# Block-diagonal attention scores on 32x32 tiles, row sums by TensorE, one range check, and a re-tuned schedule

**Chip, cores, metric.** One core of one Trainium2 chip. The metric is device time in microseconds (us), lower is better. Every run also notes the mean granted clock of TensorE. A run is called slow when it lies over 1.5% above the fastest of the same kernel on that chip, and fast otherwise; ratios use fast runs.

## The reference

```python
# x [4, 12480, 128] f32, inducing [32, 128] f32
def mab(q, kv):
    s = (q @ kv.transpose(0, 2, 1)) / sqrt(128)
    a = exp(s - s.max(-1, keepdims=True))
    a /= a.sum(-1, keepdims=True) + 1e-09
    return a @ kv
h = mab(I, x)            # 32 queries pool all 12480 tokens of a batch
y = mab(x, h)            # every token then attends to the 32 results
hid = y.reshape(49920, 128) @ w_in                        # [128, 2048]
out = (maximum(hid, 0) + alpha * minimum(hid, 0)) @ w_out # [2048, 128]
```

`h` of a batch needs all of its tokens, so each batch is gone through twice: once to pool it, once for its outputs. In between stands the **fold**: `h` and the feed-forward weights become small matrices that the outputs use. The kernel keeps the tokens of a batch on the chip between the two passes, so that `x` is read once.

## The kernel before

There are 28 chunks, seven per batch, six of 2048 tokens and one of 192. A full chunk is loaded by GpSimd's queue (f32 in memory, bf16 on arrival: the page shows 27.73 MB read and 13.83 MB in that queue's packets), turned round by VectorE in 32x32 squares ("flipped"), scored by TensorE, put through exp by ScalarE, flipped again and summed into `h`. After the fold, the same flipped tokens are scored against `h` (second scores), put through exp, and each of the chunk's four output tiles is summed from five matmuls (four of 128 columns, one of 512). An output tile is scaled either by VectorE straight from PSUM, or copied by ScalarE and scaled by GpSimd.

The order of every engine's instructions is fixed when the kernel is built. A planner inside the kernel plays the whole run with an estimated duration for each task, and the order in which tasks start in that play is the order in which the instructions are written out:

```python
RINGS = dict(xn=8, xt=14, p=7, h=1, e1=3, e1t=3, g=3, ob=4)   # buffers
CAPS = dict(A=3, S=3, F=7, O=6)                               # PSUM slots by use
SLACK, FILL, LATE, AP, BIAS = 1.5, 0.5, 70.0, 0.0, 0.8
PW, FB = 16.5, 3.0
TA, TS, TB, WL, LEAD = 3.6, 1.2, 4.2, 6, 2                    # deadlines = priorities
def dl_a(b, i): return 2.0 * i if b == 0 else 18.0 + TA * (NCK * (b - 1) + i)
# ... dl_s, dl_b alike

add(("PE", 0.02 + 4 * max(c.w / 2400, 0.06)), scores, [tf] + t_blk,
    take=["p:A"], prio=prio)      # engine and planned us, function, what it waits for,
                                  # buffers, priority
# ... Plan.play(): at each moment the ready task of the best priority starts,
#     its end is start + planned duration, and (engine, task) goes into the order
```

The parts that the change replaces (cuts marked):

```python
def blocks(a, eng, dst, flat):        # four copies put 32-row blocks on the diagonal
    rows = slice(a * M, (a + 1) * M)  # of a zeroed [128, 2, 4, 32, 2] weight tile
    copy(eng, dst[rows, :, a]..., flat[rows])

def scores(_):                        # first scores; the second use BH[r] for blkI
    for n, (bb, e) in enumerate(((0, 0), (0, 1), (1, 0), (1, 1))):
        nc.tensor.matmul(sc, blkI[:, bb, :, :, e]..., xT[:, :, bb, :, e],
                         start=(n == 0), stop=(n == 3))      # 128x128 weights, 512 columns

nc.scalar.activation(out=e1, in_=sc, func=EXP, scale=scale,
                     accum_out=esum[:, s.b, c.i : c.i + 1])  # first exp, with row sums
nc.scalar.activation(out=e2, in_=sc, func=EXP, scale=scale,
                     bias=centre[: c.p])                     # second exp

def f_flip(_):                        # fold: transpose to PSUM, then blocks() to BH[r]
    nc.vector.transpose(out=v["h4t"], in_=v["h4"]...)

def seal(_):                          # range check, once per batch
    nc.vector.tensor_scalar(out=odd, in0=odd, scalar1=~0x30003, op0=bitwise_and)
    nc.vector.tensor_reduce(out=odds[:, b : b + 1], in_=odd, op=max)
    nc.vector.memset(odd, 0)
```

The softmax here doesn't subtract the row's maximum and nothing guards it: scores larger than these inputs give would overflow.

Of the kernel before, what the change touches and what calls it, by code (L numbers as in the profile page):

```python
# [16 lines left out]
P = 128  # L17
M = 32
# [10 lines left out]
RINGS = dict(xn=8, xt=14, p=7, h=1, e1=3, e1t=3, g=3, ob=4)  # L29
CAPS = dict(A=3, S=3, F=7, O=6)  # L30
# [23 lines left out]
SLACK = 1.5  # L54
FILL = 0.5
LATE = 70.0
AP = 0.0
BIAS = 0.8


class Plan:
# [25 lines left out]
    def moved(self, now):  # L87

        while True:
            heads = {k: q[0] for k, q in self.queues.items() if q}  # L90
            busy = {k: h for k, h in heads.items() if h["begin"] <= self.clock + 1e-9}
            rate = {k: self.RATE[k] * (self.SHARE[k] if len(busy) == 2 else 1.0) for k in busy}
            events = [self.clock + h["left"] / rate[k] for k, h in busy.items()]
            events += [h["begin"] for k, h in heads.items() if k not in busy]
            nxt = min(events, default=1e9)
            to = min(nxt, now)
            for k, h in busy.items():
                h["left"] -= rate[k] * (to - self.clock)
                if h["left"] < 1.0:
                    h["end"] = to + 0.7  # L100
                    self.queues[k].pop(0)
            self.clock = max(self.clock, to)
            if nxt > now:
                return nxt

    def play(self):
# [4 lines left out]
        todo = list(self.tasks)  # L111
        self.order = order = []
        while todo:
            todo.sort(key=lambda t: (t["prio"], t["n"]))
# [3 lines left out]
            for t in todo:  # L118
                if any(d["end"] is None for d in t["deps"]):
                    continue  # L120
# [56 lines left out]
                todo.remove(t)  # L177
                order.append((choice, t))
                started = True
                break  # L180
            if not started:
                assert min(nxt) < 1e8, [(t["fn"].__name__, t["prio"], t["take"]) for t in todo if all(d["end"] is not None for d in t["deps"])][:20]
                now = min(nxt)
# [19 lines left out]
def kernel(  # L203
# [39 lines left out]
    def filler(n):  # L243
        p = ring("p")
        for _ in range(n):
            nc.tensor.matmul(
                p[:], blkI[:, 0, :, :, 0].rearrange("p a m -> p (a m)"), blkI[:].rearrange("p b a m e -> p (b a m e)"),
                start=True, stop=True,
            )
# [45 lines left out]
    blkI = const.tile([P, 2, G, M, 2], bf16, name="blkI")  # L295
    def blocks(a, eng, dst, flat):

        rows = slice(a * M, (a + 1) * M)
        copy(eng, dst[rows, :, a].rearrange("p b m e -> p b (m e)").bitcast(f32), flat[rows])
# [5 lines left out]
    def zeros(_):  # L305
        nc.vector.memset(blkI[:], 0.0)
        nc.vector.memset(esum[:], 0.0)
        nc.vector.memset(odd, 0)
        nc.vector.memset(centre[:], math.log(CENTRE))
        nc.vector.memset(mask[:], 0.0)  # L310
        for a in range(G):
            nc.vector.memset(mask[a * M : (a + 1) * M, a : a + 1], 1.0)
# [13 lines left out]
    sel = const.tile([P, M], f32, name="sel")  # L326
    sel4 = const.tile([P, G, M], f32, name="sel4")
# [12 lines left out]
    for r in range(2):  # L340
        SP.append(const.tile([P, G, G, G, CAP], bf16, name=f"sp{r}"))
        P0.append(const.tile([P, KC, M], bf16, name=f"p0{r}"))
        ZB.append(const.tile([P, C], bf16, name=f"zb{r}"))
        WB.append(const.tile([P, G, C], bf16, name=f"wb{r}"))
        BH.append(const.tile([P, 2, G, M, 2], bf16, name=f"bh{r}"))
# [6 lines left out]
    def small_dve(_):  # L352
# [4 lines left out]
        nc.vector.tensor_copy(out=sel4b[:], in_=sel4[:])  # L357
        nc.vector.tensor_copy(out=iota[:], in_=iota_i[:])
        nc.vector.memset(ident1[:], 1.0)
        nc.vector.tensor_copy(out=ident1[:, :M], in_=ident[:M, :M])  # L360
        nc.vector.memset(ones_b[:], 1.0)
# [8 lines left out]
        for r in range(2):  # L370
            nc.vector.memset(BH[r][:], 0.0)
            nc.vector.memset(P0[r][:], 0.0)
            nc.vector.memset(SP[r][:], 0.0)
# [8 lines left out]
    esum = keep.tile([P, B, NCK], f32, name="esum")  # L382
    odd = slots["h"][0][:, C : C + M * NK // 2].bitcast(i32)

    scratch = slots["h"][0][:, C + M * NK // 2 :].rearrange("p (n k) -> p n k", k=KC)
    one16 = scratch[:, 0]
    odds = keep.tile([P, B], f32, name="odds")
    centre = keep.tile([P, 1], f32, name="centre")
# [15 lines left out]
    PW = 16.5  # L404
    FB = 3.0
    OB = 0.42
    TA, TS, TB, WL, LEAD = 3.6, 1.2, 4.2, 6, 2
# [29 lines left out]
    def pool_chunk(s, c, i):  # L437
# [18 lines left out]
        def scores(_):  # L456
            v["sc"] = ring("p", [P, c.w])
            for n, (bb, e) in enumerate(((0, 0), (0, 1), (1, 0), (1, 1))):
                nc.tensor.matmul(  # L459
                    v["sc"][: c.p, :],  # L460
                    blkI[: c.p, bb, : c.na, :, e].rearrange("p a m -> p (a m)"),
                    s.xT[c.i][: c.p, : c.nk, bb, :, e],
                    start=(n == 0), stop=(n == 3),
                )

        def exps(_):
# [4 lines left out]
                func=EXP, scale=scale, accum_out=esum[: c.p, s.b, c.i : c.i + 1],  # L471
# [9 lines left out]
        def sums(_):  # L481
            if c.i == 0:
                s.h = ring("h")[:, :C]
            for k in range(c.nk):
                q = k % G
                nc.tensor.matmul(  # L486
                    s.h[q * M : (q + 1) * M, :],
# [3 lines left out]
                    stop=(c.i == NCK - 1 and k + G >= c.nk) or (c.i == NCK - 2 and k + G >= c.nk and q >= chunks[-1].nk),  # L491
                )
# [6 lines left out]
        te = add(("ACT", 0.27 + act(c.w)[1]), exps, [ts], take=["e1"], give=[("p", ts)], prio=prio)  # L499
        tt = add(dve(c.w // 2), flip_e, [te], take=["e1t"], give=[("e1", te)], prio=prio)  # L500
        return add(
            ("PE", 0.08 + 0.017 * c.nk), sums, [tt, s.pooled], take=["h"] if c.i == 0 else [],
# [4 lines left out]
    def fold_batch(b):  # L507
# [12 lines left out]
        def f_hp(_):  # L520
            nc.scalar.copy(out=sm("hp", [P, C + 1], f32)[:, :C], in_=s.h[:])

        def f_es(_):
            nc.vector.tensor_reduce(
                out=v["hp"][:, C : C + 1], in_=esum[:, b, :], axis=AX.X, op=ALU.add
# [15 lines left out]
        def f_flip(_):  # L541
            v["h4t"] = dtile([P, C // 2], "h4t")
            nc.vector.transpose(out=v["h4t"], in_=v["h4"][:].bitcast(f32))
# [45 lines left out]
        t = t_c = add(act(C), f_hp, [s.pooled], give=[("h", s.first_sum)], prio=prio)  # L589
        t_e = add(("DVE", 0.12), f_es, [s.pooled, t_c], prio=prio)  # L590
# [6 lines left out]
        for n in range(2):  # L597
# [4 lines left out]
        t = t_ft = add(("DVE", 0.24), f_flip, [t_n], take=["p:F"], prio=prio + 0.05)  # L602
        t_b = [
            add({"DVE": 0.2, "ACT": 0.25},
                lambda e, a=a: blocks(a, e, BH[r], v["h4t"].rearrange("p (b m) -> p b m", b=2)),
                [t] + s.free_h, prio=prio + 0.05)
            for a in range(G)
        ]
        add(("NONE", 0.0), lambda _: None, t_b, give=[("p", t_ft)], prio=prio)
# [4 lines left out]
        def second(c, pr):  # L614
            w = {}

            def scores(_):
                w["sc"] = ring("p", [P, c.w])
                for n, (bb, e) in enumerate(((0, 0), (0, 1), (1, 0), (1, 1))):
                    nc.tensor.matmul(  # L620
                        w["sc"][: c.p, :],
                        BH[r][: c.p, bb, : c.na, :, e].rearrange("p a m -> p (a m)"),
                        s.xT[c.i][: c.p, : c.nk, bb, :, e],
                        start=(n == 0), stop=(n == 3),
                    )

            def exps(_):
# [3 lines left out]
                    func=EXP, scale=scale, bias=centre[: c.p],  # L631
# [14 lines left out]
            te = add(("ACT", 0.12 + act(c.w)[1]), exps, [ts], give=[("p", ts)], prio=pr)  # L646
            tx = add(dve(c.w // 2), extent, [te, bt[b - 1].sealed if b else None], prio=pr + XP)
# [3 lines left out]
        XP = 40.0  # L651
# [5 lines left out]

        def seal(_):
            nc.vector.tensor_scalar(
                out=odd, in0=odd, scalar1=~0x30003, scalar2=None, op0=ALU.bitwise_and  # L660
            )
            nc.vector.tensor_reduce(
                out=odds[:, b : b + 1], in_=odd, axis=AX.X, op=ALU.max, apply_absolute_value=True
            )
            nc.vector.memset(odd, 0)

        s.sealed = add(("DVE", 1.0), seal, s.extents, prio=dl_s(b, NCK - 1) + XP)

# [276 lines left out]
    for b in range(B):  # L945
        bt[b].loads, bt[b].flips, bt[b].pooled = [], [], None
    t_z = add(("DVE", 0.9), zeros, prio=-9)
    t = add(("ACT", 1.8), ind_load, prio=-10, bytes=2 ** 16)
    t = add(("DVE", 0.47), ind_flip, [t], prio=-8)
    t_blk = [  # L950
        add(("DVE", 0.2) if a % 2 else ("ACT", 0.25), lambda e, a=a: blocks(a, e, blkI, ind_t[:].rearrange("p b m e -> p b (m e)").bitcast(f32)),
            [t, t_z], prio=-7)
        for a in range(G)
    ]
# [14 lines left out]
    def check(_):  # L969

        top = keep.tile([P, B], f32, name="top")
        nc.vector.tensor_scalar(
            out=top[:], in0=odds[:], scalar1=0.0, scalar2=None, op0=ALU.is_gt
        )
        tp = ring("p", [P, B])
        nc.tensor.matmul(tp[:], ones_f[:], top[:], start=True, stop=True)
        nc.vector.tensor_tensor(
            out=flags_f[:, :B], in0=flags_f[:, :B], in1=tp[0:1, :], op=ALU.max
# [7 lines left out]
        ("DVE", 2.5), check, [t for s in bt for t in (s.sealed, s.flagged)], take=["p:F"], prio=dl_b(B - 1, NCK),  # L986
# [105 lines left out]
```

## Time and profile before

| | |
|---|---|
| time | 155.67 us, median of 3 (155.38 to 156.37) |
| profiled execution | span 153.5 us, clock 0.894, fast |
| bytes | 27.73 MB read, 25.56 MB written |

The first line of the profile's page gives each engine's busy time, its share of the span and its instructions:

```profile
PE 106.9 (70%) x1637; PEld 58.1 (38%) x1640; DVE 103.7 (68%) x284; ACT 83.1 (54%) x214; POOL 92.1 (60%) x114
```

No engine is near full over the whole run. The prediction below shows why that average says little: to about 102 us the transfers are the limit (their share is 1.05 from 2 to 94 us and 0.99 up to 102), after it they are not (0.66 up to 127 us). What the prediction looked at less closely, and what also belong here, is GpSimd's timeline in that second part. Columns are start, length, engine, line, operation, number of instructions, and in brackets the idle time before them with what ended it:

```profile
107.28 1.05 POOL L879 TENSOR_TENSOR ob<-ob,rd 128x512 f32<-128x512 f32 x1 [2.12 <-ACT ob L866]
109.51 3.06 POOL L879 TENSOR_TENSOR ob<-ob,rd 128x512 f32<-128x512 f32 x3 [1.19 <-ACT ob L866]
114.50 2.06 POOL L879 TENSOR_TENSOR ob<-ob,rd 128x512 f32<-128x512 f32 x2 [1.92 <-ACT ob L866]
117.52 3.06 POOL L879 TENSOR_TENSOR ob<-ob,rd 128x512 f32<-128x512 f32 x3 [0.97 <-ACT ob L866]
122.62 3.06 POOL L879 TENSOR_TENSOR ob<-ob,rd 128x512 f32<-128x512 f32 x3 [2.03 <-ACT ob L866]
```

While batch 3 is folded, batch 2's outputs reach GpSimd one, two or three tiles at a time, with a wait of 1 to 2 us for ScalarE's copy ahead of each group.

### The profile page before, as it was taken

What the parts mean: (1) busy time and instruction counts of PE and PEld (TensorE: products, weight loads), DVE (VectorE), ACT (ScalarE), POOL (GpSimd) and SP (SyncE); (2) the same over time, 40 slices, a digit from 0 to 9 for tenths busy, and PEclk for the clock granted to TensorE, in tenths of its full rate; (3) what the DMA queues carried; (4) which work ended last, traced back from release to release, by engine and by line L of the source; (5) the groups of instructions that cost most, each with busy time, mean ns of one, the idle gap of its engine ahead of it and who ended that gap; (6) DMA issues with size and microseconds to landing.
All of it is one profiled execution on the core that took longest, in us unless ns stands there. A gap on an engine that the chain in (4) does not pass through costs nothing. (4 is left out here: it accounts for less than half of the span.)

```text
span 153.5 us, 4238 instructions
## 1 busy us (share of the span) xinstructions
PE 106.9 (70%) x1637; PEld 58.1 (38%) x1640; DVE 103.7 (68%) x284; ACT 83.1 (54%) x214; POOL 92.1 (60%) x114
## 2 busy tenths in 40 slices
PE   0039987999974977968668999996596993446100
PEld 0013434554542343625336545453353553334100
DVE  2089874898968687378898989786958857432400
ACT  3012523646884677654565868875547588364400
POOL 7910137611799669780098597514647478799900
PEclk9999999999999699999999879999969999555555
DMA  3999999999999999999999999994966648769991
GB/s 35 209 217 210 212 211 217 210 217 208 216 213 259 393 389 215 354 354 209 215 215 213 331 300 403 391 343 176 341 238 258 255 152 293 297 267 357 353 360 55
DMA packets 18057, 39.78 MB, mean 259 GB/s; under 512 B 1136, under 2 KB 2416, under 8 KB 18032
## 3 DMA queue, kind: packets, MB, share of 16 engines
q0 software_dynamic: 4192, 13.83, 46.6%
q1 hardware_dynamic: 13648, 25.57, 44.8%
q8 instruction: 14, 0.23, 0.6%
q10 hardware_dynamic: 192, 0.07, 0.3%
q14 instruction: 11, 0.09, 0.2%
HBM read 27.73 MB, written 25.56 MB: 347 GB/s over the span
## 5 line engine op out<-in xcount | busy, mean ns | idle before, releaser
L879 POOL TENSOR_TENSOR ob<-ob,rd 128x512 f32<-128x512 f32 (+1 forms) x73 | 71.0, 1002 | 31.3 <-ACT ob L866 27.8
L866 ACT COPY ob<-p 128x512 f32<-128x512 f32 (+1 forms) x73 | 36.4, 573 | 9.4 <-POOL ob L879 5.3
L459 PE MATMUL p<-xt,blkI 128*128 128x512 bf16 (+1 forms) x112 | 29.1, 388 | 14.8 <-DVE xt L450 14.1
L450 DVE STREAM_TRANSPOSE xt<-xn 128x1024 f32<-128x1024 f32 (+1 forms) x28 | 30.0, 1081 | 5.2 <-DMA xn<-in_x_dram 5.1
L443 POOL DMA_DIRECT2D xn<-in_x_dram x28 | 15.4, 555 | 21.4 <-PE h L486 8.4
L620 PE MATMUL p<-xt,bh 128*128 128x512 bf16 (+1 forms) x112 | 26.2, 364 | 2.7 <-DVE bh L287 2.4
L468 ACT ACTIVATE e<-p 128x512 bf16<-128x512 f32 (+1 forms) x28 | 15.3, 548 | 18.2 <-PE p L459 14.8
L864 DVE TENSOR_TENSOR ob<-p,rd 128x512 f32<-128x512 f32 (+1 forms) x35 | 19.8, 590 | 5.3 <-PE p L849 4.3
L628 ACT ACTIVATE e<-p,centre 128x512 bf16<-128x512 f32 (+1 forms) x28 | 17.5, 633 | 10.7 <-PE p L620 10.3
L459 PEld LDWEIGHTS <-blkI 128*128 128x128 bf16 (+1 forms) x112 | 10.0, 105 | 24.7 <-ACT blkI L285 9.0
L844 PE MATMUL p<-zb,e 32*128 32x128 bf16 (+1 forms) x396 | 12.4, 238 | 8.6 <-ACT g L836 8.3
L620 PEld LDWEIGHTS <-bh 128*128 128x128 bf16 (+1 forms) x112 | 9.7, 103 | 11.8 <-DVE bh L287 2.6
L486 PE MATMUL h<-xn,e1t 128*32 128x128 bf16 x392 | 10.0, 222 | 5.4 <-DVE h L637 3.2
L844 PEld LDWEIGHTS <-e 32*128 32x128 bf16 (+1 forms) x396 | 7.5, 101 | 15.8 <-issue 14.7
L637 DVE SCALAR_TENSOR_TENSOR h<-e,h 128x256 int32<-128x256 int32 (+1 forms) x28 | 10.7, 381 | 3.6 <-PE h L486 1.8
L476 DVE STREAM_TRANSPOSE e1t<-e 128x256 f32<-128x256 f32 (+1 forms) x28 | 10.6, 382 | 3.2 <-ACT e L468 3.1
L829 DVE RECIPROCAL rd<-p 128x16 f32<-128x16 f32 (+1 forms) x28 | 6.5, 231 | 8.5 <-ACT ob L866 4.1
L849 PE MATMUL p<-wb,g 32*128 32x512 bf16 (+1 forms) x108 | 11.9, 415 | 0.0
L818 PE MATMUL p<-e,sp 128*128 128x128 bf16 (+1 forms) x100 | 11.4, 238 | 0.0
L836 ACT ACTIVATE g<-p 128x128 bf16<-128x128 f32 (+1 forms) x28 | 8.0, 285 | 6.2 <-DVE rd L829 5.7
L486 PEld LDWEIGHTS <-e1t 128*32 128x32 bf16 x392 | 6.2, 96 | 11.4 <-DVE e1t L476 6.9
L818 PEld LDWEIGHTS <-sp 128*128 128x128 bf16 (+1 forms) x100 | 6.7, 104 | 8.0 <-issue 7.1
(109 smaller groups left out, 112.5 us busy)
## 6 DMA issues: line engine op xcount, KB each, us to landing
out_dram<-ob SPq DMA_DIRECT2D x24, 1024.0 KB, 6.3
xn<-in_x_dram POOLq DMA_DIRECT2D x24, 512.0 KB, 13.0
w_in_b<-in_moe_w_in_dram POOLq DMA_DIRECT2D x1, 512.0 KB, 15.4
WO<-in_moe_w_out_dram POOLq DMA_DIRECT2D x1, 512.0 KB, 17.3
out_dram<-ob SPq DMA_DIRECT2D x4, 96.0 KB, 5.5
xn<-in_x_dram POOLq DMA_DIRECT2D x4, 48.0 KB, 10.3
ind<-in_inducing_dram ACTq DMA_DIRECT2D x4, 16.0 KB, 2.8
al<-in_moe_alpha_dram SPq DMA_DIRECT2D x1, 8.0 KB, 2.0
```

Source lines behind the costliest of these rows:

```text
L443: nc.gpsimd.dma_start(out=v["xn"][: c.p, : c.nk, :], in_=x[s.b, c.t0 : c.t0 + c.n, :].rearrange("(p j) c -> p j c", p=c.p),)
L450: nc.vector.transpose(out=xT[: c.p, : c.nk].rearrange("p k b j e -> p (k b j e)").bitcast(f32), in_=v["xn"][: c.p, : c.nk, :].bitcast(f32),)
L459: nc.tensor.matmul(v["sc"][: c.p, :], blkI[: c.p, bb, : c.na, :, e].rearrange("p a m -> p (a m)"), s.xT[c.i][: c.p, : c.nk, bb, :, e], sta ...
L468: nc.scalar.activation(out=v["e1"][: c.p, : c.w].rearrange("p (K j e) -> p K j e", j=M, e=2), in_=v["sc"][: c.p, :].rearrange("p (K e j) - ...
L486: nc.tensor.matmul(s.h[q * M : (q + 1) * M, :], v["e1t"][: c.p, k // 2, :, k % 2], v["xn"][: c.p, k, :], start=(c.i == 0 and k < G), stop= ...
L620: nc.tensor.matmul(w["sc"][: c.p, :], BH[r][: c.p, bb, : c.na, :, e].rearrange("p a m -> p (a m)"), s.xT[c.i][: c.p, : c.nk, bb, :, e], st ...
L628: nc.scalar.activation(out=s.e2[: c.p, c.off : c.off + c.w].rearrange("p (r j k) -> p r j k", j=M, k=c.nkk), in_=w["sc"][: c.p, :].rearran ...
L818: nc.tensor.matmul(hh[:, : c.po], SP[r][: c.p, q].rearrange("p a q f -> p (a q f)"), e2(q), start=(q == 0), stop=(q == c.nq - 1),)
L844: nc.tensor.matmul(v["o"][a][: c.po, q * C : (q + 1) * C], e2(q, rows[a]), ZB[r][rows[a], :], start=(q == 0), stop=False,)
L864: nc.vector.tensor_tensor(out=ob, in0=o, in1=spread(rd), op=ALU.mult)
L866: nc.scalar.copy(out=ob, in_=o)
L879: nc.gpsimd.tensor_tensor(out=ob, in0=ob, in1=spread(s.rd[: c.po, c.i, : c.nq, a]), op=ALU.mult,)
```

## The change

The intent: take work off ScalarE and VectorE, drop the four copies that stand in the fold between `h` and the second scores, and choose the planner's constants anew for the new set of tasks. The diff, cut to its core:

```diff
-RINGS = dict(xn=8, xt=14, p=7, h=1, e1=3, e1t=3, g=3, ob=4)
-CAPS = dict(A=3, S=3, F=7, O=6)
+RINGS = dict(xn=12, xt=10, p=7, h=1, e1=3, e1t=3, g=3, ob=5)
+CAPS = dict(A=2, S=2, F=7, O=5)
-SLACK = 1.5          # LATE 70.0, AP 0.0, BIAS 0.8
+SLACK = 0.7          # LATE 90.0, AP -0.2, BIAS 0.4
-    PW = 16.5        # FB 3.0, XP 40.0
+    PW = 12.5        # FB 10.0, XP 10.0
-    TA, TS, TB, WL, LEAD = 3.6, 1.2, 4.2, 6, 2
+    TA, TS, TB, WL, LEAD = 4.0, 0.6, 4.2, 10, 0
+    def scores_of(sc, c, rows_t, xT):        # rows_t: ind_t, or BH[r] of the fold
+        for n, (bb, e) in enumerate(((0, 0), (0, 1), (1, 0), (1, 1))):
+            for a in range(c.na):
+                rows = slice(a * M, (a + 1) * M)
+                nc.tensor.matmul(
+                    sc[rows, :], rows_t[rows, bb, :, e], xT[rows, : c.nk, bb, :, e],
+                    start=(n == 0), stop=(n == 3))
-                func=EXP, scale=scale, accum_out=esum[: c.p, s.b, c.i : c.i + 1],
+                func=EXP, scale=scale,
+            for k in range(c.nk // 2):           # row sums, in sums()
+                nc.tensor.matmul(
+                    e_all[q * M : (q + 1) * M, :], ones_b[: c.p, :M],
+                    v["e1t"][: c.p, k]..., start=False, ...)
-            nc.vector.transpose(out=v["h4t"], in_=v["h4"][:].bitcast(f32))
+            nc.vector.transpose(out=BH[r][:]..., in_=v["h4"][:].bitcast(f32))
-        t_b = [add(..., blocks(...), [t] + s.free_h) for a in range(G)]
+        t_b = [add(("DVE", 0.24), f_flip, [t_n] + s.free_h, prio=prio + 0.05)]
-                    func=EXP, scale=scale, bias=centre[: c.p],
+                    func=EXP, scale=scale, bias=math.log(CENTRE),
-        def seal(_): ...                         # per batch: gone
+    # check(_), once at the end, does the and, the max and the compare
```

(The planner's code was also made faster on the host; that does not change what it decides.)

## The prediction

> **What bounds the kernel now.** I read the slices of the page first (where the transfers stop being the limit), then the table of stretches (which engine fills each), then the timeline of the last 50 us, then the groups for the durations of what is removed or added.
>
> ```profile
> DMA  3999999999999999999999999994966648769991
> GB/s 35 209 217 210 212 211 217 210 217 208 216 213 259 393 389 215 354 354 209 215 215 213 331 300 403 391 343 176 341 238 258 255 152 293 297 267 357 353 360 55
> ```
>
> A slice is 153.5/40 = 3.84 us. From about 2 us to slice 27 (about 102 us) the transfer engines are full. A load shows as some 212 GB/s because it is f32 in memory and bf16 on arrival: it reads twice that, 424 GB/s. A pure store runs at some 393. So until 102 us the kernel moves bytes, and a faster engine earns nothing there directly. The bytes stay the same: 27.73 MB read at 424 GB/s is 65.4 us and 25.56 MB written at 394 is 64.9 us, 130.3 us in all. With about 2 us of start and some 7 us from the last result to the end this makes an estimated floor near 139 us of span. The span is 153.5, so some 14 us are to be had, and they lie after 102 us.
>
> ```profile
> core 0: us, PE busy (x) PEld busy (x) DVE busy (x) ACT busy (x) POOL busy (x), PEclk, DMA share, GB/s
> 2.00:94.00 92.00, 71.02 (x1074) 37.30 (x1078) 69.78 (x181) 51.00 (x137) 54.75 (x72) 0.96 1.05 251
> 94.00:102.00 8.00, 7.81 (x90) 3.66 (x88) 6.34 (x18) 5.94 (x14) 4.12 (x5) 1.00 0.99 378
> 102.00:127.00 25.00, 19.92 (x346) 11.70 (x334) 18.56 (x58) 16.25 (x41) 14.34 (x14) 0.93 0.66 245
> 127.00:146.00 19.00, 8.10 (x142) 5.46 (x141) 8.17 (x22) 9.88 (x25) 17.90 (x19) 0.61 0.84 317
> 146.00:153.50 7.50, 0.00 (x0) 0.00 (x0) 0.00 (x0) 0.00 (x0) 0.00 (x0) 0.50 0.60 205
> ```
>
> The last two working stretches have different limits. From 127 to 146 us (outputs of batch 3) GpSimd is busy 17.90 of 19.00 us: the plan gave it three of the four tiles of nearly every 1 MB chunk, while VectorE does one and idles. From 102 to 127 us no engine is above 80% (TensorE 19.92 of 25): this stretch is a chain of waits around the fold of batch 3, with transfers at 245 GB/s.
>
> ```profile
> 108.90 0.26 DVE L543 STREAM_TRANSPOSE p<-h 128x64 f32<-128x64 f32 x1
> 110.39 0.46 DVE L287 COPY bh<-p 32x64 f32<-32x64 f32 x2
> 110.91 1.89 PE L620 MATMUL p<-xt,bh 128*128 128x512 bf16 x4 [1.56 <-DVE bh L287]
> 134.05 11.81 POOL L879 TENSOR_TENSOR ob<-ob,rd 128x512 f32<-128x512 f32 x13 [0.83 <-ACT ob L866]
> ```
>
> The transpose of the folded queries ends at 109.16 us, but its four copies into the zero-padded block matrix go on to 110.85, and TensorE stands 1.56 us before the second scores. Those four matmuls then take 1.89 us instead of 1.03, as the clock has just been halved.
>
> [...] the second exp, with `centre` as bias, takes 688 ns, the first 603. [...]
>
> ```profile
> 45.82:49.24 3.42, 1.19 (x20) 0.63 (x20) 2.72 (x6) 1.64 (x6) 3.42 (x5) 1.00 1.04 244
> 49.24:52.65 3.41, 3.41 (x33) 1.41 (x32) 2.28 (x6) 2.83 (x7) 2.17 (x3) 0.50 1.03 377
> ```
>
> [...] The new scores put four row tiles into one bank, though each into other partitions. Row tiles of this kernel go to four banks today, so its trace is silent on it.
>
> **The change part by part.**
>
> ```profile
> L468 ACT ACTIVATION_READ_ACCUMULATOR e<-p 128x1 f32 x24 | 4.9, 203 | 0.0
> L628 ACT ACTIVATE e<-p,centre 128x512 bf16<-128x512 f32 x24 | 16.5, 688 | 10.6 <-PE p L620 10.3
> L659 DVE TENSOR_SCALAR h<-h 128x256 int32<-128x256 int32 x4 | 1.7, 433 | 0.6 <-ACT hp L521 0.4
> L486 PE MATMUL h<-xn,e1t 128*32 128x128 bf16 x384 | 9.2, 222 | 5.4 <-DVE h L637 3.2 <-DVE e1t L476 1.8 <-DVE h L567 0.3
> ```
>
> *ScalarE.* The sum beside the first exp goes: 28 readouts of 203 ns, 5.7 us. The bias becomes a constant: 24 x 85 ns, 2.0 us. Four block copies go, 0.9 us. In all 8.6 of 83 us.
>
> *VectorE.* Three of the four range checks go: (433 + 424 + 272) ns x 3 = 3.4 us. 16 block copies go, 16 x 0.21 = 3.4 us less what ScalarE had. The sum of the row sums grows from 117 to an estimated 300 ns, four times. In all about -6 of 104 us.
>
> *TensorE.* Both scores become 16 matmuls of 32x32 per chunk. If the four diagonal tiles run side by side, the streaming is the same four passes of 512 columns, and a chunk's scores stay at 1.03 us. For this speaks that 16 row-tiled matmuls of 128 columns (the outputs) take 0.40 us and 16 column-tiled ones (the sums) 0.41, both about four passes of 56 ns and a fill. The new row sums add 8 column-tiled matmuls of 64 columns: two passes of 27 ns and their weight loads, about 0.12 us a chunk, 3 us in all. TensorE's matmul count rises by 2 x 28 x 12 + 196 = 868.
>
> *Order and buffers.* By the order of the built kernel, 12 chunks are scaled on GpSimd ahead of the last load's issue, 9 before, with loads and stores mixed more evenly. Batch 3 gives GpSimd 15 full tiles and two small ones, where it had 17 and two. There are 12 load buffers for 8, five output buffers for four, but ten flipped tiles for 14.
>
> **What of it lies on the path.** Before 102 us, nothing but the order. After it:
> - batch 3's outputs: two full tiles less on the engine that fills the stretch, 2 x 1.02 = 2.0 us. Transfers need 2.66 us per chunk, 16 us for the stretch, so 1.8 of this may stay;
> - batch 3's fold: the transpose writes the score weights directly, so the second scores may start at 109.2 instead of 110.91, less 0.2 for the longer row sum: 1.5 us;
> - the half clock from 110.67 to 114.08 us cost 0.86 (scores) + 0.21 + 0.26 + 0.16 (the output group) = 1.5 us. [...] I count half of it, 0.8 us;
> - a fifth output buffer: one more finished chunk stands ready as the loads end and goes out at 2.66 us, not at the 3.75 us a chunk of the time after 102 us (49 us for 13.6 MB): 1.1 us;
> - the new order otherwise, with 8.6 and 6 us less work on ScalarE and VectorE, of which about a quarter falls after 102 us: I choose 1.5 us;
> - against it: slices with loads and stores mixed moved 350 to 390 GB/s, pure ones 394 to 424. More mixing I put at +1.0 us.
> The sum is -1.8 - 1.5 - 0.8 - 1.1 - 1.5 + 1.0 = -5.7 us, so 155.67 - 5.7 = 150.0 us.
>
> **The rivals.**
> 1. *The transfers take it all back.* The gain in engine time lies in the full-transfer part, and only ten flipped tiles let batch b+1 get at most three chunks ahead of batch b's second scores. Flips then wait, load buffers stay held, and the transfer engines run dry in the middle. For it: already now GpSimd's load issues stood 15.5 us in waits for buffers; against it: 12 load buffers keep more queued. This makes 153 to 156 us.
> 2. *The clock.* A diagonal pass lights a quarter of the array that a full pass does. [...] TensorE falls to half speed for much of the run: 48 chunk scores at 1.89 instead of 1.03 us are 41 us more, and TensorE's 107 us become some 150 and the bound. This makes 160 to 175 us. [...] I give it one chance in eight.
> 3. *No overlap.* If tiles of one bank are serialised, 16 passes of 0.215 us take 3.4 us a chunk, and the kernel lies over 220 us. Two chances in a hundred.
> 4. *It goes better.* If the stretch from 102 us becomes transfer-bound throughout (13.6 MB at 394 GB/s are 34.6 us for 49), 14 us go: 142 us.
>
> **Range and chances.** The sum says 150.0; the middle is as uncertain as the order's share, so 145.5 to 156.0 holds rivals 1 and half of 4. Faster by over 2% means under 152.6 us: 0.67. Within 2%: 0.20, mostly rival 1. Slower: 0.13, nearly all rival 2.
>
> **What would show it.** Right: no accumulator readouts, second exp near 603 ns, a chunk's scores still 1.03 us at full clock, transfers full to about 100 us, then more than 278 GB/s on average up to the last store, batch 3's GpSimd stretch shorter by 2 us, no wait on copies before the second scores. Wrong: half clock in the middle of the run or score groups near 1.9 us (rival 2), 3.4 us (rival 3), or gaps in the transfer row before 100 us with flips waiting on second scores (rival 1).

## The result

| | median | all runs | state |
|---|---|---|---|
| before | 155.53 | 156.37, 155.38, 155.67, 155.40 | all fast |
| after | 152.79 | 149.65, 150.99 / 154.58, 156.57 | two fast / two slow |

A ratio is the mean time of one kernel's fast runs over that of the other's fast runs of the same rounds, so it is not quite the ratio of the medians. Here it is **0.9646** (95%: 0.956 to 0.9732). The fast runs average 150.3 us where 150.0 was predicted.

One caution goes with that. The changed kernel's times spread over 4.6% within one set, the old kernel's over 0.6% on that chip and 1.5 to 2.7% on three others. Leaving out the slow runs flatters the kernel that spreads more: over all runs the ratio of means is 0.982 here and 0.973 in the repetition below. "Slow" is only a distance from the fastest run. The granted clocks do not part the two (fast: 0.923, 0.902, 0.903, 0.890; slow: 0.907, 0.861, 0.890, 0.886, 0.916, 0.904).

Both profiled executions of the changed kernel, this one (span 152.3 us) and that of the repetition (150.4), are slow ones. I read them for what work is done in which order, and take sizes, where I can, from the fast profile of experiment `e7_first_full` (148.7 us), whose order is the same. The page's rows after; in the 40 slices the DMA digit is the transfer engines' busy share in tenths:

```profile
PE 110.2 (72%) x2474; PEld 60.5 (40%) x2474; DVE 94.9 (62%) x251; ACT 77.6 (51%) x190; POOL 93.4 (61%) x119
DMA  3999999999999999999999999998199888689991
GB/s 37 200 216 211 215 210 214 215 216 213 209 226 214 343 273 336 404 284 247 220 251 242 371 268 271 363 281 315 66 377 374 306 298 289 238 305 386 376 363 37
```

Transfers are full up to slice 27 as before, and after it, but for slice 28, much fuller than before. The table of stretches, whose columns are those of the prediction's table, puts numbers on that:

```profile
102.00:127.00 25.00, 22.84 (x522) 12.69 (x510) 17.29 (x53) 18.33 (x51) 18.53 (x23) 0.93 0.81 296
127.00:145.00 18.00, 8.08 (x142) 5.52 (x142) 8.39 (x22) 8.58 (x22) 15.85 (x17) 0.60 0.86 315
```

From 102 to 127 us the kernel moves 296 GB/s instead of 245, and GpSimd works 18.53 us instead of 14.34. The groups of instructions by shape (out<-in, count | busy us, mean ns), first before, then after:

```profile
L459 PE MATMUL p<-xt,blkI 128*128 128x512 bf16 x96 | 27.7, 418 | 14.4 <-DVE xt L450 14.1 <-ACT ob L866 0.2
L620 PE MATMUL p<-xt,bh 128*128 128x512 bf16 x96 | 24.9, 389 | 2.7 <-DVE bh L287 2.4 <-DVE ob L864 0.2
```

```profile
L317 PE MATMUL p<-xt,bh 32*32 32x512 bf16 x384 | 28.0, 406 | 3.2 <-issue 2.9 <-DVE wb L770 0.2
L317 PE MATMUL p<-xt,ind_t 32*32 32x512 bf16 x384 | 26.1, 388 | 12.4 <-DVE xt L472 11.6 <-DVE ob L869 0.5 <-issue 0.3
L644 ACT ACTIVATE e<-p 128x512 bf16<-128x512 f32 x24 | 14.4, 598 | 12.2 <-PE p L317 12.0
```

Four times as many matmuls take the same time (54.1 us for both scores, 52.6 before, half-clock stretches included). A full chunk at full clock takes 1.05 us where it took 1.03 (first line before, second after):

```profile
19.88 1.03 PE L459 MATMUL p<-xt,blkI 128*128 128x512 bf16 x4 [0.72 <-DVE xt L450]
96.75 1.05 PE L317 MATMUL p<-xt,ind_t 32*32 32x512 bf16 x16
```

So the four diagonal tiles do run side by side, and the prediction's rivals 2 (the clock; its mean is 0.907 here and was 0.894) and 3 (no overlap) are out. The second exp fell from 688 to 598 ns (603 expected), and ScalarE has no accumulator readout left. "<-issue" is new in these lines; it comes back below.

**Where the time went.** The kernel has three marks that can be read from the timelines: the last sum matmul of batch 3 (pooling done), GpSimd's first output tile of batch 3, and its last.

| us | pooling done | to batch 3's first output | to its last output | to the end | span |
|---|---|---|---|---|---|
| before (fast) | 106.1 | 21.1 | 18.7 | 7.6 | 153.5 |
| after (slow) | 108.9 | 18.0 | 16.9 | 8.5 | 152.3 |
| repetition (slow) | 107.3 | 17.7 | 16.9 | 8.6 | 150.4 |
| same order, first scores 128x128 (fast) | 107.1 | 16.4 | 16.9 | 8.3 | 148.7 |

Pooling ends 1 to 3 us later, the stretch after it is 3.1 to 4.7 us shorter, and the last two together are about 1 us shorter. The two executions of the changed kernel differ by 1.6 us in the first column and by 0.3 in all the rest: most of their difference arises before pooling is done.

In the middle stretch GpSimd's timeline after reads:

```profile
105.94 10.11 POOL L884 TENSOR_TENSOR ob<-ob,rd 128x512 f32<-128x512 f32 x10 [2.25 <-ACT ob L871]
118.43 6.08 POOL L884 TENSOR_TENSOR ob<-ob,rd 128x512 f32<-128x512 f32 x6 [2.38 <-ACT ob L871]
124.73 1.11 POOL L884 TENSOR_TENSOR ob<-ob,rd 64x128 f32<-64x128 f32 x3 [0.22 <-ACT ob L871]
```

Ten tiles run without a gap through the fold of batch 3. Between the first two marks GpSimd is busy 12.29 of 21.05 us before and 14.32 of 17.96 after: its idle time falls from 8.8 to 3.6 us. (In `e7_first_full`, fast and in the same order, it is busy 14.36 of 16.43 us.) The difference lies in the order. Before, one output group (at 108.21 us) stood between pooling and the second scores; then TensorE went into the scores, and the next output group came only after them (the scores at 110.91 us are in the prediction):

```profile
112.73 0.61 PE L844 MATMUL p<-zb,e 32*128 32x128 bf16 x16
```

After, two output groups (at 109.08 and 111.59 us) stand ahead of the scores, and so do the fold's 16 matmuls and the next group's first part:

```profile
108.73 0.19 PE L512 MATMUL h<-e1t,ones_b 96*32 96x64 bf16 x1
...
111.56 0.24 DVE L569 STREAM_TRANSPOSE bh<-h 128x64 f32<-128x64 f32 x1
111.59 0.18 PE L575 MATMUL p<-ident,h 32*128 32x33 bf16 x1 [1.00 <-DVE h L563]
111.59 0.41 PE L849 MATMUL p<-zb,e 32*128 32x128 bf16 x16
...
112.15 1.17 PE L585 MATMUL p<-hT,w_in_b 128*128 128x33 bf16 x16
...
113.56 3.59 PE L317 MATMUL p<-xt,bh 32*32 32x512 bf16 x32
```

Here pooling is done at 108.92 us and the score weights are ready at 111.80, 2.9 us later, where it took 4.8 before. But the scores start at 113.56, 4.6 us after pooling, as late as before (4.8). The fold did become shorter; the planner spent the time on outputs.

### The profile page after: what moved, and what is told of

Same layout as the page of the kernel before. It is cut to its first block, busy times and chain, and to the rows that moved or that the text cites. A ratio compares the mean times of both kernels' runs of the same rounds, so it can differ in the third digit from the quotient of the medians.

```text
span 152.3 us, 5852 instructions
## 1 busy us (share of the span) xinstructions
PE 110.2 (72%) x2474; PEld 60.5 (40%) x2474; DVE 94.9 (62%) x251; ACT 77.6 (51%) x190; POOL 93.4 (61%) x119
## 5 line engine op out<-in xcount | busy, mean ns | idle before, releaser
L884 POOL TENSOR_TENSOR ob<-ob,rd 128x512 f32<-128x512 f32 (+1 forms) x78 | 72.2, 954 | 33.9 <-ACT ob L871 33.8
L871 ACT COPY ob<-p 128x512 f32<-128x512 f32 (+1 forms) x78 | 37.7, 549 | 15.2 <-PE p L854 9.6
L317 PE MATMUL p<-xt,ind_t 32*32 32x512 bf16 (+1 forms) x432 | 27.3, 366 | 12.6 <-DVE xt L472 11.6
L317 PE MATMUL p<-xt,bh 32*32 32x512 bf16 (+1 forms) x432 | 29.0, 381 | 3.2 <-issue 2.9
L484 ACT ACTIVATE e<-p 128x512 bf16<-128x512 f32 (+1 forms) x28 | 15.1, 551 | 22.4 <-PE p L317 20.3
L644 ACT ACTIVATE e<-p 128x512 bf16<-128x512 f32 (+1 forms) x28 | 15.2, 546 | 12.2 <-PE p L317 12.0
L869 DVE TENSOR_TENSOR ob<-p,rd 128x512 f32<-128x512 f32 (+1 forms) x30 | 19.1, 652 | 0.5 <-PE p L854 0.5
L317 PEld LDWEIGHTS <-ind_t 32*32 32x32 bf16 x432 | 9.3, 92 | 22.8 <-DVE ind_t L336 9.5
L317 PEld LDWEIGHTS <-bh 32*32 32x32 bf16 x432 | 10.4, 93 | 11.1 <-issue 4.2
L823 PE MATMUL p<-e,sp 128*128 128x128 bf16 (+1 forms) x100 | 10.9, 231 | 0.0
## 6 DMA issues: line engine op xcount, KB each, us to landing
w_in_b<-in_moe_w_in_dram POOLq DMA_DIRECT2D x1, 512.0 KB, 16.4
```

The lines of the kernel that those rows point to most:

```text
L317: nc.tensor.matmul(sc[rows, :], rows_t[rows, bb, :, e], xT[rows, : c.nk, bb, :, e], start=(n == 0), stop=(n == 3),)
L484: nc.scalar.activation(out=v["e1"][: c.p, : c.w].rearrange("p (K j e) -> p K j e", j=M, e=2), in_=v["sc"][: c.p, :].rearrange("p (K e j) - ...
L644: nc.scalar.activation(out=s.e2[: c.p, c.off : c.off + c.w].rearrange("p (r j k) -> p r j k", j=M, k=c.nkk), in_=w["sc"][: c.p, :].rearran ...
L823: nc.tensor.matmul(hh[:, : c.po], SP[r][: c.p, q].rearrange("p a q f -> p (a q f)"), e2(q), start=(q == 0), stop=(q == c.nq - 1),)
L869: nc.vector.tensor_tensor(out=ob, in0=o, in1=spread(rd), op=ALU.mult)
L871: nc.scalar.copy(out=ob, in_=o)
```

## The experiments

Two ways of building were used. **Re-planned**: the planner runs on the edited kernel, so everything may move. **Order frozen**: the planner is given the tasks and durations of one kernel, and the edited instructions are put into the functions of those tasks, so every engine keeps that kernel's order. An order takes its buffer counts with it: the new order also means 12 load, ten flipped and five output buffers. The notes of expectations were written before each run.

**Is the gain there again?** `e1_after_again` is the changed kernel, unedited, on another chip.

> The changed kernel again, unaltered, for more times and a profile in the fast state. All theories: fast runs near 150.3 us (149.6 to 151), some runs 2.5% or more above. Theory F (instruction fetch): a fast profile also shows TensorE standing 0.4 to 1.8 us inside groups of matmuls with no semaphore to wait for, in sum 6 to 9 us against under 0.5 us in the kernel before, each just after a 16 KB packet on the instruction queue; and the slow runs differ by where these stands and the half-clock windows fall. Rival: the stands belong to the slow run only.

Measured: 152.64 us median (150.01 to 155.66) against 156.97 for before; ratio 0.9669 (0.9555 to 0.9783). The gain and the wide spread are both there again.

### Parts or order?

`e2_plan_only` is the kernel before with nothing but the changed constants, re-planned:

```diff
-RINGS = dict(xn=8, xt=14, ..., ob=4)      # and CAPS, SLACK, LATE, AP, BIAS,
+RINGS = dict(xn=12, xt=10, ..., ob=5)     # PW, FB, TA..LEAD, XP: all as changed
```

> The kernel before with only the changed constants: buffer counts, caps, and the plan's priorities and weights. Theory P (the gain is order and buffers, as engine time before about 100 us is hidden behind the transfers): 150 to 152 us. Theory W (the gain is the removed engine work and the shorter fold): 154.5 to 156 us. No stands of TensorE inside groups, as the instructions are those of before.

Measured: 157.66 us, ratio 1.0083 (0.9981 to 1.0185), which neither theory expected.

`e3_parts_only` is the changed kernel with the old constants, re-planned:

```diff
-RINGS = dict(xn=12, xt=10, ..., ob=5)     # and the others: all back
+RINGS = dict(xn=8, xt=14, ..., ob=4)
```

> The changed instructions with the old constants: 8 load buffers, 14 flipped tiles, four output buffers, old priorities. Theory P: 154 to 157 us. Theory W: 150 to 152 us. Theory F: stands inside TensorE's groups remain, 5 to 9 us in sum.

Measured: 164.53 us, ratio 1.0524 (1.043 to 1.0617). The new instructions under the old constants are 5% slower than before; again neither theory expected that.

`e5_old_parts_new_order` freezes the changed kernel's order and puts all old instructions back into it; `e6_new_parts_old_order` freezes the order of before and puts all new instructions in:

```diff
# e5, on the changed kernel; no add() is touched
+    def full_scores(sc, c, rows_t, xT): ...       # four 128x128 matmuls
-            scores_of(v["sc"], c, ind_t, s.xT[c.i])
+            full_scores(v["sc"], c, blkI, s.xT[c.i])
-                func=EXP, scale=scale,
+                func=EXP, scale=scale, accum_out=esum[...],
+            for a in range(G):                     # in f_flip
+                blocks(a, "DVE", BH[r], flat...)   # + seal(), bias operand; - row sums
# e6, on the kernel before: the same replacements the other way
```

> The changed kernel's order on every engine held fast (its plan's task costs and priorities untouched), but with the instructions of the kernel before inside the tasks: full 128x128 scores on block weights with the copies, accumulator readouts and bias operand on ScalarE, a range check per batch, no row sums on TensorE. Theory O (the new order alone brings the gain): under 152.5 us or 0.975 of before. Theory W (the removed work brings it): 0.99 to 1.01. Theory I (order and work fit each other; neither brings it alone): 0.985 to 1.03, with slips of the order where the old, longer instructions stand.

Measured: 158.47 us, ratio 1.0092 (1.0001 to 1.0183). This run is tainted: my copies read the flipped `h` from SBUF, where the kernel before reads it from PSUM, and in the four folds they took 2.70, 0.78, 0.79 and 1.36 us, some 2.3 us more than 16 copies of 0.21 us in all, or 1.5%. Taking off just these durations gives near 0.995, but that is no safe correction. In batch 0's fold the copies took 2.70 us beside a GpSimd instruction of 3.61 us, and TensorE waited 2.83 us for the copies:

```profile
25.08 3.61 POOL L963 TENSOR_TENSOR W<-WO,om 128x2048 bf16<-128x2048 bf16 x1 [5.06 <-DMA WO<-in_moe_w_out_dram]
26.71 2.70 DVE L302 COPY bh<-h4t 32x64 f32<-32x64 f32 x4
29.48 1.81 PE L326 MATMUL p<-xt,bh 128*128 128x512 bf16 x4 [2.83 <-DVE bh L302]
```

GpSimd's first output tile then came at 42.4 us (38.7 in `e7_first_full`, 39.9 in the slow profile of the changed kernel), and the transfers fell to 73 GB/s in slice 11. So what the old instructions alone cost in the new order stays open in this run.

> The other half: the order of the kernel before held fast, with all the new instructions in its tasks (32x32 scores, row sums on TensorE, no readouts, constant bias, no block copies, one range check). Theory O: 0.99 to 1.01 of before. Theory W: 0.96 to 0.975. Theory I: 0.985 to 1.03. Theory F (instruction fetch): stands inside TensorE's groups appear here too, 4 to 9 us in sum, which the kernel before hasn't.

Measured: 160.31 us, ratio 1.0113 (1.0009 to 1.0216).

So, with frozen orders:

| ratio to before | old instructions | new instructions |
|---|---|---|
| old order | 1.000 | 1.011 |
| new order | 1.009 (tainted) | 0.965 and 0.967 |

As measured, neither half earns anything to speak of; together they earn 3.4%. For the new instructions in the old order that is shown. For the old instructions in the new order it rests on the tainted `e5` and, without a taint, on `e11` below, in which the range checks alone take the gain back. The marks in the profiles show where the time lies:

| us | pooling done | from there to the end |
|---|---|---|
| before | 106.1 | 47.4 |
| old instructions, new constants (e2, slow) | 116.0 | 43.6 |
| old instructions, new order (e5, fast) | 110.0 | 44.2 |
| new instructions, old order (e6, slow) | 110.0 | 48.5 |
| new instructions, old constants (e3, fast) | 117.8 | 43.0 |
| changed kernel (two slow executions) | 108.9, 107.3 | 43.4, 43.1 |

At the first mark about 12.9 MB are still to be moved in before, e5, e6 and the changed kernel (by the packets of their traces), so these rests can be compared. In e2 it is 11.9 and in e3 11.0 MB: their rests are short in part because more outputs had gone out by then.

The new **order** shortens the part after pooling by 3 to 4 us, whichever instructions it carries. With the old instructions pooling ends 4 us later, which takes that back; how much of this is the taint of e5 is open. With the new **instructions**, and without the taint, pooling ends 1 to 3 us sooner than in e5. Why the new instructions in the old order delay pooling by 4 us is not settled; that profile has TensorE standing 2.5 us within groups (see below), but no run takes that alone away.

### Single parts

`e4_full_array` is the changed kernel with 128x128 scores, block copies and all, re-planned:

```diff
-                nc.tensor.matmul(sc[rows, :], rows_t[rows, bb, :, e], ...)
+            nc.tensor.matmul(sc[: c.p, :], rows_t[: c.p, bb, : c.na, :, e]..., ...)
-        t_b = [add(("DVE", 0.24), f_flip, [t_n] + s.free_h, ...)]
+        t_b = [add({"DVE": 0.2, "ACT": 0.25}, blocks..., [t] + s.free_h, ...) for a in range(G)]
```

> The changed kernel with only the 32x32 scores undone: four 128x128 matmuls per chunk on zero-padded block weights, with the copies that build them; row sums on TensorE, one range check and the new constants stay. Theory F: the stands inside groups fall under 1.5 us in sum; if they lie on the path the time falls to 147 to 149 us and the spread between runs shrinks; if hidden behind the transfers it stays within 1% of 150.3. Theory W: block copies and the later second scores come back on the fold's path, 1 to 2 us each where transfers do not hide it, so 151 to 153 us.

Measured: 158.22 us (155.49 to 161.52), ratio 0.9984 (0.988 to 1.0086). The whole gain is gone. But the order moved too, so this alone cannot say which half did it: pooling ends at 111.6 us and the rest takes 48.1, so the good second part is lost with the order. The next two runs hold the order fixed.

`e7_first_full` keeps the changed kernel's order and puts only the **first** scores back on a 128x128 block weight, which is built once at the start:

```diff
+        for a in range(G):                              # in ind_flip
+            blocks(a, "DVE", blkI, ind_t...)
-            scores_of(v["sc"], c, ind_t, s.xT[c.i])
+            full_scores(v["sc"], c, blkI, s.xT[c.i])
```

> The changed kernel in its own order with only the first scores back on four 128x128 matmuls with a block weight built once at the start: 672 TensorE instructions fewer. Theory F: the stands inside groups fall from 6 to 8 us to under 2.5; if they cost time on the path the kernel gets to 147.5 to 149 us and varies less; if the transfers hide them, 0.99 to 1.01 of the changed kernel.

Measured: 150.80 us (149.62 to 152.74), four of five runs fast, ratio 0.9598 (0.9523 to 0.9673). So the 32x32 form of the first scores earns nothing: leaving it out is as fast in the fast runs, within the intervals, and the kernel spreads less (four of five runs fast, against four of ten). It is the best version I ran, and that it beats the changed kernel is only suggested, as the intervals overlap and the chips differ. What the 32x32 form can be worth must then lie in the fold, where it saves copies; no clean run here shows that.

`e9_second_full` keeps the order and puts only the **second** scores back, with the copies in the fold's transpose task:

```diff
-            nc.vector.transpose(out=BH[r][:]..., in_=v["h4"]...)
+            flat = sm("h4t", [P, C // 2], f32)
+            nc.vector.transpose(out=flat[:], in_=v["h4"]...)
+            for a in range(G):
+                blocks(a, "DVE", BH[r], flat...)
-                scores_of(w["sc"], c, BH[r], s.xT[c.i])
+                full_scores(w["sc"], c, BH[r], s.xT[c.i])
```

> The changed kernel's order held, only the second scores back on 128x128 block weights, with the transpose and its four copies in the fold's task. My step 'the second scores may start 1.5 us sooner': 1.5 us come back for batch 3 and some for the others where the transfers run dry, 0.975 to 0.985 of before (the changed kernel: 0.965 to 0.967). If this is the part that made the old instructions miss in the new order, 0.99 or more. If the fold isn't on the path: 0.965 or, by fewer instruction fetches, 0.96.

Measured: 165.27 us, ratio 1.0607 (1.0516 to 1.0698). That is far more than four copies of 0.2 us in each of four folds, and the timeline of batch 0's fold shows where a part of it arises:

```profile
25.92 3.61 POOL L956 TENSOR_TENSOR W<-WO,om 128x2048 bf16<-128x2048 bf16 x1 [5.70 <-DVE rt L575]
26.59 3.67 DVE L302 COPY bh<-h4t 32x64 f32<-32x64 f32 x4
...
30.32 1.89 PE L325 MATMUL p<-xt,bh 128*128 128x512 bf16 x4 [3.80 <-DVE bh L302]
```

The copies, four of 0.2 us from PSUM in the kernel before, here take 3.67 us, until 30.26 us, shortly after a GpSimd instruction of 3.61 us has ended at 29.53. TensorE waits 3.80 us for them and then takes 1.89 us for a chunk's scores, where the kernel before takes 1.03 at full clock. In batch 3's fold three of the copies take 3.00 us, from 119.53 us, while GpSimd works on output tiles from 119.42 to 123.49. In the kernel before, two copies from PSUM took 0.46 us (at 110.39) beside GpSimd's output tiles (109.51 to 112.57). That the copies from SBUF are slow because GpSimd works at the same time is my inference from these times; no run takes GpSimd's work away. My variant thus brought in slow copies that neither original has, and says nothing on the size of the fold's term. In the four folds the copies took 3.67, 1.87, 0.77 and 3.20 us, some 6 us more than 16 copies of 0.2 us (an estimate from these durations). The run is some 15 us slower than the changed kernel; where the rest of it arises I did not trace. It warns against correcting e5, which has the same copies, by their durations alone.

`e10_readouts_back` keeps the order and gives ScalarE its readouts and bias operand back (5.7 + 2.0 us); `e11_checks_back` does the same for the range check per batch (3 x 1.13 us of VectorE):

```diff
# e10
-                func=EXP, scale=scale,
+                func=EXP, scale=scale, accum_out=esum[: c.p, s.b, c.i : c.i + 1],
-                    func=EXP, scale=scale, bias=math.log(CENTRE),
+                    func=EXP, scale=scale, bias=centre[: c.p],
# e11, after the last extent() of a batch
+                    nc.vector.tensor_scalar(out=odd, in0=odd, scalar1=~0x30003, ...)
+                    nc.vector.tensor_reduce(out=odds[:, b : b + 1], in_=odd, ...)
+                    nc.vector.memset(odd, 0)
```

> The order held, only ScalarE's work back: 28 accumulator readouts of 203 ns and the bias operand, 24 times 85 ns, 7.8 us in all; the sums are not used. If ScalarE's work matters for the new order: 0.985 or more. My step 'a quarter of it falls after 102 us and part of that counts': 0.972 to 0.978. If hidden: 0.965 to 0.97.

Measured: 152.86 us, ratio 0.9776 (0.9692 to 0.986). Against 0.9669 that is 1.1% of fast runs; over all runs the two kernels stand at 0.975 and 0.973. So ScalarE's 7.8 us are worth somewhere between 0.2 and 1.1%, which these runs do not resolve.

> The order held, only the range check per batch back: 1.13 us of VectorE three times more. If it matters: 0.98 or more; if hidden: 0.965 to 0.97.

Measured: 155.90 us, ratio 0.9973 (0.9892 to 1.0054), 3% above 0.9669 (1.9% over all runs). In all, 3.4 us of VectorE cost 3 to 4.7 us of time. The timeline shows the spot in one fold:

```profile
58.01 0.43 DVE L659 TENSOR_SCALAR h<-h 128x256 int32<-128x256 int32 x1
58.48 0.42 DVE L662 TENSOR_REDUCE odds<-h 128x1 f32<-128x256 int32 x1
59.03 0.27 DVE L665 MEMSET h<- 128x256 int32 x1
59.21 0.15 DVE L562 RECIPROCAL rt<-p 128x1 f32<-128x1 f32 x1
59.36 0.41 PE L502 MATMUL h<-xn,e1t 128*32 128x128 bf16 x16 [1.24 <-DVE rt L562]
```

The check stands ahead of the fold's reciprocal, and TensorE's 1.24 us wait is one for that reciprocal. Work that "VectorE has room for" (62% busy) sits in the chain of the fold, because the frozen order puts it there.

### Clock and buffers

`e8_fill1` doubles the idle matmuls that the planner puts into TensorE's gaps, meant to hold the clock:

```diff
-FILL = 0.5
+FILL = 1.0
```

> The changed kernel with FILL 1.0 for 0.5: the plan, with the same order, puts twice as many idle matmuls into its own gaps. Theory C (the half-clock windows make the slow runs): mean clock rises above 0.93 and the slow runs, over 152.5 us, vanish or get rare. Rival: the plan's gaps are not where the real ones are, so the clock stays at 0.89 to 0.92 and the times and their spread as they are, or 0.5 us worse.

Measured: 155.01 us, ratio 0.9863 (0.9788 to 0.9939), so slower than the changed kernel, with clocks of 0.886 to 0.909, no higher than its own. As the clock did not rise, the run does not test the theory that a higher clock would bring more; it shows that these idle matmuls (35 in the profile for 16) cost and do not help. Against clock as the cause of the spread speaks only that the clocks of fast and slow runs overlap.

`e12_ob4` takes the fifth output buffer away, re-planned:

```diff
-RINGS = dict(xn=12, xt=10, ..., ob=5)
+RINGS = dict(xn=12, xt=10, ..., ob=4)
```

> The changed kernel with four output buffers for five, so the plan orders anew (the order is not held). My step 'a fifth buffer is worth 1.1 us': 0.972 to 0.978. If the order found for five buffers is a narrow fit, anything up to 1.0 or more, with other order on the engines; if neither: 0.965 to 0.97.

Measured: 162.29 us, ratio 1.0371 (1.0295 to 1.0447), that is 7% above the changed kernel. These are some 11 us where I had put 1.1 on the buffer, and the planner found another, worse order around four buffers (pooling done at 112.1 us, then 48.5). As a measure of the buffer alone it is inconclusive. As a measure of how narrow the good order is, it stands beside e3 and e4.

### Standing without a cause in the waits

TensorE's list of waits (what it waited for: us in all, times, longest) has lines that the kernel before has none of:

```profile
PE p L849 <- issue: 3.8, 4, 1.4
PE p L317 <- issue: 3.5, 4, 1.8
PE h L512 <- issue: 1.2, 1, 1.2
```

These are 8.5 us in which TensorE waited for nothing that the profile shows (6.5 in the repetition, 5.5 in e7, 2.2 to 6.2 in e3, e6 and e8 to e12, none in before and e2). One of them, in the repetition:

```profile
56.39 1.05 PE L317 MATMUL p<-xt,bh 32*32 32x512 bf16 x15
58.94 0.37 PE L317 MATMUL p<-xt,bh 32*32 32x512 bf16 x1 [1.50 <-issue]
...
61.29 1.89 PE L317 MATMUL p<-xt,bh 32*32 32x512 bf16 x16
```

Fifteen of a chunk's 16 matmuls run, the sixteenth comes 1.5 us later, and after it the next chunk's scores take 1.89 us. The page has a row for instruction transfers (packets, MB, share of the transfer engines), before and after:

```profile
q8 instruction: 14, 0.23, 0.6%
```

```profile
q8 instruction: 21, 0.34, 0.8%
```

Seven packets of 16 KB more; TensorE has 1671 more instructions (matmuls and weight loads), so one more packet to some 240 instructions, an estimate from these two differences. For e7, with 643 instructions fewer than that, the row shows 18. And in this profile and the repetition's each such stand ended 2.2 to 2.6 us after the last such packet had begun. So TensorE may have run out of instructions while more were brought beside full transfers. That is an inference: no run changes the number of these packets and nothing else, and e7, from which I expected under 2.5 us of such stands, had 5.5. What they cost in time stays open; it is not the whole gain or loss of any kernel here, as the changed kernel wins in spite of 8.5 us.

## Why the prediction was right, and where it was not

The total was right: -5.7 us predicted, -5.2 measured in the fast runs (155.5 to 150.3). By stretches it was near too: +1.0 for the pooling part, -4.9 for the middle (fold, clock, buffer, order), -1.8 for batch 3's outputs, against +1.0, -4.7 and -1.1 in e7's fast profile. (The changed kernel's own profiles, both slow, give +1.2 to +2.8, -3.1 to -3.4 and about -0.9.) But the steps behind the middle number were partly wrong: a term that failed was made up for by one that was chosen without evidence, so that the total came so close is in part luck.

- **What bounds it: right.** The gain lies after pooling, and the part before it, which transfers fill, got slightly slower.
- **GpSimd's tail (-1.8): right in work, a little large in time.** The stretch went from 18.7 to 16.9 us. But the time from its end to the end of the run grew from 7.6 to 8.3-8.6, so about 1.0 stays.
- **The fold (-1.5): failed.** The step "the second scores may start at 109.2 instead of 110.91" took the old order for granted. The weights came 1.9 us sooner after pooling, and the scores no sooner (4.6 us after pooling, 4.8 before), as the plan puts one more output group and the fold's matmuls ahead of them.
- **The half clock (-0.8): not confirmed.** That half of its cost would go was an estimate; what had brought it on is not shown. In this profile the stretch is still there, from 113.6 to 117.0 us (clock 0.50), and the two chunks scored in it took 3.59 us instead of 2.1; the repetition has one at 110.6. Both are slow runs. In e7's fast profile the clock is full from 102.1 to 126.0 us. Whether fast runs of the changed kernel have the stretch, no profile shows.
- **What stood in their place:** the order of the outputs. GpSimd's idle time between pooling and batch 3's outputs fell by 5.1 us. In e5, which has the new order but the copies still in its fold, this stretch takes 18.5 us, against 21.1 before and 18.0 after: most of the gain there comes with the order and not with the shorter fold. Of that gain I had only "the order otherwise" (-1.5), by choice, with no view behind it. I had read that stretch from TensorE's and VectorE's rows; GpSimd's own timeline, shown above, held the answer already.
- **The fifth buffer (-1.1): not measured.** The run that took it away changed the order.
- **Less work (within -1.5): not additive.** On the page ScalarE's busy time fell by 5.5 us, where 8.6 was predicted, and VectorE's by 8.8, where 6 was; putting the readouts and the operand back in e10 added 4.2 us, not 7.8. VectorE's checks alone come to 3 to 4.7 us in this order, ScalarE's part to 0.2-1.1%; and all the new instructions in the old order cost 1.1%. A sum of durations cannot give that.
- **Mixing of loads and stores (+1.0): right in size.** Pooling ends 1.0 to 2.8 us later. By the packets of the old kernel's trace, with loads counted as read, the full slices with both moved 316 to 407 GB/s (mean 384), those of loads alone 419 to 428 and of stores alone 386 to 401. That mixing is the cause is not shown; the stands of TensorE fall into that part too.
- **A count.** TensorE's matmuls rose by 837, not 868: a chunk of 192 tokens has three row blocks, so its scores take 12 small matmuls and not 16. Nothing hangs on it.
- **Rivals.** Waiting flips (1) did not appear: transfers stay full to slice 27. Rivals 2 and 3 are refuted by the 1.05 us a chunk.

The fast and slow runs of the changed kernel, 5% apart, I did not foresee, and their cause stays open. The mean clock does not part them; the difference of the two profiled executions arises before pooling ends.

## What to carry to other kernels

When a static order is tuned for a set of tasks, instructions and order are one thing: test a part with the order frozen, and doubt any "one constant only" run that was re-planned. A copy taken out of a chain shortens the chain only if the next thing in the engine's order is what waited for it; else the time goes to whatever stands there, which may be just as well. Read the stretch that you want to shorten from the timeline of every engine that feeds the last one, not only from the one that waits most visibly.

## What the traces show beside the question

- **Clock and share of the array.** In the changed kernel's window from 96.55 to 99.96 us TensorE was busy 2.27 us, 2.06 of them in 32x32 tiles of which four use a quarter of the array (some 0.7 us in all if those are weighed by area, an estimate from these two times), and the clock stayed at 1.00, in the next 3.41 us too. In the old kernel's window from 45.83 to 49.24 us it was busy 1.19 us with the whole array in use, and in the next 3.41 us the clock was 0.50. So a small share of the array did not bring the clock down here. No threshold of busy time parts the windows: the old kernel kept the clock after 1.85 us (from 76.55) and lost it after 2.67 (from 83.37). What halves it is not shown.
- **Four row tiles in one output tile.** Four diagonal 32x32 tiles wrote one PSUM tile of 128x512 f32, each into its own 32 partitions, with results that passed the check and at the speed of the 128x128 form (1.05 against 1.03 us a chunk).
- **Stands of TensorE.** They lasted 0.3 to 2.7 us at a time, 2.2 to 8.5 us in a run, in kernels with 16 small matmuls to one score or both; the link to the instruction packets is inferred from their times.
